# Folding and piece ends moved from VectorE to GpSimd, and one more border step with the border order, in a fused Fourier filter and SiLU network

## The chip, the core and the metric

The kernel runs on one core of one Trainium2 chip. Its time is the device time of one execution in microseconds (us), as the median of several runs. Before the change this is 2573.56 us (three runs, 2570.03 to 2574.13). The engines of the core work beside each other, each through its own instructions in order: PE (TensorE, matrix products), DVE (VectorE) and POOL (GpSimd) for elementwise work, ACT (ScalarE) for copies and SiLU, SP for issuing DMAs. POOL issues DMAs too, and such an issue stands in the same queue as its arithmetic.

## The reference

```python
X = np.fft.rfft(x, axis=1)                    # x: 8 x 3008 x 256, f32
y = np.fft.irfft(X * (filt_r + 1j * filt_i)[None], n=3008, axis=1)
h = y.reshape(8 * 3008, 256) @ w_in           # w_in: 256 x 2048
out = (h / (1 + np.exp(-h))) @ w_out          # w_out: 2048 x 256
```

Each of the 8 batches is filtered along its 3008 positions in the frequency domain. The 24064 tokens that result go through a two-layer network with SiLU.

## The kernel before

**The network is the frame.** A batch is cut into 6 pairs of token blocks (256, 256 and 240 columns, twice). For a pair, the 2048 hidden units are worked off in 8 steps (`jp` 0 to 7) of 256, so a batch has 48 steps and the kernel 384. Both matrix products of a step use a 2 by 2 scheme with seven block products in place of eight. `hidden(step)` issues the seven products with w_in (L957), ACT copies intermediate sums out of PSUM (L965, L972, L978) and does SiLU (L961), DVE combines (all through the helper `combine`, L928). `project(step)` issues the seven products with w_out (L1020) one step later (`LAG`), into four accumulators in PSUM, a0 to a3. At the end of a pair `drain` copies these to SBUF (L1038, L1040), POOL makes seven additions on them (L928, tile s), and SP stores them.

A step has 8 rounds. In each round PE gets one product of `hidden` and then one of `project` (round 5 has none of the former, round 7 none of the latter). Each product is two PE instructions. What follows calls the products by their weights: A11, A12, S2, S1, S3, then A22 and S4 for `hidden`. DVE's own work in a step is, in its order:

- g0: the sum of A12's result and a copy (it reads PSUM and SBUF), in round 1
- g6 and g7, in `finish`: differences within the tile g, for the step before (both operands in SBUF, 256 columns each); `project`'s sixth and seventh product, in rounds 5 and 6 of this step, read them
- g2, after S3, reads the bank that S4 will add to in round 7
- g1, after S4; the next step's A12 writes the bank that g1 reads
- g4 and g5 in one instruction: a difference within g, 512 columns, both operands in SBUF

**The filter is woven in.** The next batch's transform and filter and inverse transform are cut into pieces, and each is put by hand at a step and a round (`put(step, round, piece)`). After each round, pieces due by then are issued; they go into the engines' queues behind that round's work. For batches 2 to 7, `plan` and `plan_two` do this. Their times are relative to `at`, the batch's own first step (48 times its number):

- `fold(f, k)` (L486 to L499), three times (f 0 to 2) in four parts: sums and differences of x with its reversed copy, operands and results in SBUF, 120 partitions. Parts 0 and 1 are one instruction of 1024 columns each, parts 2 and 3 two of 512 each. f 0 is put at steps -68 to -66, f 1 at -60 to -58, f 2 at -52 to -50. The result is read by `stage1_fold` (PE, L509) at -64, -56 and -48, round 7, and `evict_fold` (ACT) and `pairs_fold` (DVE L444, L445; DMAs by POOL, L528) follow it.
- `load_fold` brings x_all in through SP nine steps ahead of f 0's product, and for f 1 and 2 after the previous product has read x_all. The fold's buffer "u" is single; for f 0 the last `multiply_two` (L586) of the batch before must have read it.
- `forward_two`, `multiply_two`, `add_two` (L591, L592), then `plan_inverse` for the groups g 0, 2 and 4: `inverse_two` (PE, L604), `even_two` (ACT), `rows_two` (DVE, two instructions on L616, one operand in PSUM), `ends_two` (DVE, L621 and L622, 512 columns each, both operands in SBUF), and two DMAs by POOL (L625). Each group has two such pieces, i 0 and 1. The inverse of a group is put at steps -32, -24 and -16 of its batch; its ends are at 2 and 3 steps after.
- `tokens(pair)` (DVE, three instructions "ty", SBUF to SBUF) is put once a pair. For the fifth pair of a batch it is due at step 26, round 6, which is the step of the ends of the next batch's group 2, piece 0 (26, round 5).

**Border steps.** At the first step of a pair (`jp` 0), filter pieces use accumulators that the pair before has just left. The set `joined` names steps at which `project` takes another order: A11, A12, S1, S3 before S4, so that a2 and a3 come late. At other borders S4 (which writes a2) comes first. The set `opened` issues two products of `project` ahead of `hidden`.

Of the kernel before, what the change touches and what calls it, by code (L numbers as in the profile page):

```python
# [49 lines left out]
ALU = mybir.AluOpType  # L50
# [177 lines left out]
def kernel(  # L228
# [9 lines left out]
    nc = tc.nc  # L238
# [95 lines left out]
    def spectral(b):  # L334
# [151 lines left out]
        def fold(f, k):  # L486

            used = slice(0, 120)
            if k == 0:
                us["f"] = upool.tile([128, 2, 512], FP32, name=f"uf_{b}_{f}", tag="u")  # L490
            xt, ut = x_all[used], us["f"][used]
            todo = (((ut, xt[:, :, 0], xt[:, :, 1], ALU.add),),
                    ((xt[:, :, 1], xt[:, :, 0], xt[:, :, 1], ALU.subtract),),
                    ((xt[:, 0, 0], ut[:, 0], ut[:, 1], ALU.add),
                     (xt[:, 1, 0], ut[:, 0], ut[:, 1], ALU.subtract)),
                    ((ut[:, 0], xt[:, 0, 1], xt[:, 1, 1], ALU.subtract),
                     (ut[:, 1], xt[:, 0, 1], xt[:, 1, 1], ALU.add)))
            for out, in0, in1, op in todo[k]:
                nc.vector.tensor_tensor(out=out, in0=in0, in1=in1, op=op)  # L499

        def stage1_fold(f):
            ut = us.pop("f")
# [115 lines left out]
        def ends_two(g, i):  # L618
            qt = halves[g][1][i]
            low = opool.tile([128, 2, C], FP32, name=f"low_{b}_{g}_{i}", tag="o")  # L620
            nc.vector.tensor_tensor(out=low, in0=qt[:, 0], in1=qt[:, 1], op=ALU.add)  # L621
            nc.vector.tensor_tensor(out=qt[:, 0], in0=qt[:, 0], in1=qt[:, 1], op=ALU.subtract)  # L622
            a0 = 8 * g + 8 * i
            for end, part in ((0, low), (1, qt[:, 0])):
                nc.gpsimd.dma_start(out=d2[a0:a0 + 8, 16 * end:16 * end + 16], in_=part)  # L625
# [146 lines left out]
    joined, opened = set(), set()  # L772
    ACCS, HIDDEN = (2, 3), ("x", "yz")

    def put(step, rnd, piece, *args):

        pending.append((step + rnd / ROUNDS, len(pending), lambda: piece(*args)))
# [3 lines left out]
    def plan(b, part):  # L781

        at = STEPS * b

        if b == 1:
            for u in range(2, 8):
                put(at + u - 49, 3, part["stage1"], u)
        else:
            put(at - 80, 0, part["reverse_x"])
            for f, step, load, places, ends in (  # L790
                    (0, -64, -73, ((-68, 3), (-68, 5), (-67, 5), (-66, 5)), ((1, 0), (1, 3))),
                    (1, -56, -63, ((-60, 3), (-60, 5), (-59, 5), (-58, 5)), ((1, 3), (1, 5))),
                    (2, -48, -55, ((-52, 3), (-52, 5), (-51, 5), (-50, 5)), ((1, 3), (1, 5)))):
                put(at + load, 0, part["load_fold"], f)
                for k, (fold_step, rnd) in enumerate(places):
                    put(at + fold_step, rnd, part["fold"], f, k)
                put(at + step, 7, part["stage1_fold"], f)
                put(at + step, 7, part["evict_fold"], f)
                for q, (after, rnd) in enumerate(ends):
                    put(at + step + after, rnd, part["pairs_fold"], f, q)  # L800
            opened.add(at - 63)
            for u, step in ((6, -46), (7, -45)):
                put(at - 47, 0, part["load_x"], u)
                put(at + step, 5, part["sums"], u)
            open_step(at - 44, (part["stage1"], 6), (part["stage1"], 7))
            put(at - 44, 3, part["pairs_t1"], 0)
            put(at - 44, 5, part["pairs_t1"], 1)
            return plan_two(b, part)
        put(at - 38, 0, part["load_t2"], 0)
        put(at - 38, 0, part["load_t2"], 1)  # L810
        for g, places in enumerate((
                ((-36, 3), (-36, 5), (-35, 3), (-35, 5), (-34, 5)),
                ((-35, 6), (-34, 3), (-33, 3), (-33, 5), (-32, 1)),
                ((-32, 7), (-31, 0), (-31, 2), (-28, 5), (-27, 2)),
                ((-27, 3), (-27, 5), (-26, 3), (-25, 3), (-24, 3)),
                ((-24, 7), (-23, 0), (-23, 2), (-20, 2), (-20, 5)),
                ((-20, 3), (-19, 3), (-19, 5), (-18, 3), (-18, 5)))):
            pieces = (("forward", g), ("multiply", g, 0), ("multiply", g, 1), ("add", g, 0), ("add", g, 1))
            for (step, rnd), (piece, *args) in zip(places, pieces):
                if piece != "forward" or g in (1, 3, 5):  # L820
                    put(at + step, rnd, part[piece], *args)
        open_step(at - 36, *last_part[0](5), (part["forward"], 0))
        for g, step in ((0, -32), (2, -24), (4, -16)):
            put(at + step, 7, part["inverse"], g, 2)
            if g < 4:
                pending.append((at + step + 7 / ROUNDS, 10 ** 6 + 9, lambda g=g: part["forward"](g + 2, ACCS)))
                joined.add(at + step)
            put(at + step, 7, part["even"], g, 0, 2)
            put(at + step, 7, part["even"], g, 1, 2)
            put(at + step + 1, 5, part["rows"], g, 0, 2)  # L830
            put(at + step + 2, 3, part["rows"], g, 1, 2)
        put(at - 14, 5, part["load_t4"], 0)
        put(at - 14, 5, part["load_t4"], 1)
        open_step(at - 10, *alone(part, 0), (part["stage3"], 1))
        put(at - 10, 3, part["evict_y"], 1, 0)
        put(at - 10, 5, part["evict_y"], 1, 1)
        join(at - 8, part, 2, 3)
        plan_rest(b, part)
# [11 lines left out]
    def plan_two(b, part):  # L850

        at = STEPS * b
        put(at - 42, 0, part["load_t2"], 0)
        put(at - 42, 0, part["load_t2"], 1)
        for g, step, places in (
                (0, -40, ((-39, 3), (-39, 5), (-38, 3), (-38, 5), (-37, 3), (-36, 3))),
                (2, -32, ((-31, 0), (-31, 2), (-29, 5), (-28, 3), (-28, 5), (-27, 3))),
                (4, -24, ((-23, 0), (-23, 2), (-22, 2), (-21, 5), (-20, 2), (-18, 3)))):
            if g:
                plan_inverse(at + step, part, g - 2)  # L860
                opened.add(at + step + 1)
            put(at + step, 7, part["forward_two"], g)
            put(at + step, 7, part["free_two"], g)
            pieces = (("multiply_two", 0, 0), ("multiply_two", 0, 1), ("add_two", 0),
                      ("multiply_two", 1, 0), ("multiply_two", 1, 1), ("add_two", 1))
            for (place, rnd), (piece, *args) in zip(places, pieces):
                put(at + place, rnd, part[piece], g, *args)
        plan_inverse(at - 16, part, 4)
        put(at - 12, 1, part["load_t4"], 0)
        put(at - 12, 1, part["load_t4"], 1)  # L870
        two_alone(at - 10, part, 0)
        join(at - 8, part, 2, 3)
        plan_rest(b, part)
# [7 lines left out]
    def open_step(step, *pieces):  # L881

        opened.add(step)
        for piece, *args in pieces:
            pending.append((step - 0.06, len(pending), lambda piece=piece, args=args: piece(*args)))

    def alone(part, g, home=HIDDEN):
        return (part["stage3"], g, home), (part["evict_y"], g, 1), (part["evict_y"], g, 0)
# [5 lines left out]
    def join(step, part, *gs):  # L894

        pieces = [(part["stage3"], gs[0], ACCS), (part["evict_y"], gs[0], 0)] if gs[0] is not None else []
        for g in gs[1:]:
            pieces = [*alone(part, g), *pieces]
        for k, (piece, *args) in enumerate(pieces):
            pending.append((step + 7 / ROUNDS, 10 ** 6 + k, lambda piece=piece, args=args: piece(*args)))  # L900
        if gs[0] is not None:
            put(step + 1, 0, part["evict_y"], gs[0], 1)
        joined.add(step)
# [458 lines left out]
    for b in range(1, B):  # L1362
        plan(b, second if b == 1 else spectral(b))
# [81 lines left out]
```

## Time and profile before

| What | Value |
|---|---|
| Median of 3 runs | 2573.56 us (2570.03 to 2574.13) |
| The profiled execution's own time | 2574.01 us |
| Its span (first to last instruction) | 2571.5 us |
| Granted clock of TensorE, mean | 0.996 |
| Busy: DVE, ACT, POOL | 1660.8, 1103.6, 438.5 us |
| Fold on DVE (L499), 72 of 512 columns and 36 of 1024 | 108 instructions, 90.2 us |
| Ends on DVE (L621, L622), all three groups | 72 instructions, 49.5 us |
| POOL's additions for the drains (L928, s) | 331 instructions, 256.1 us |

The busy time of an engine is the union of its instructions. A line of the timeline gives start, duration, engine, line, operation, and written tile "<-" read tiles with columns; several alike in a row are merged ("x2"). A bracket names the idle time before and who ended it. A line of the waits gives the waiting engine and instruction, who ended the wait, the total in us, the number of times and the longest.

### The profile page before, as it was taken

What the parts mean: (1) busy time and instruction counts of PE and PEld (TensorE: products, weight loads), DVE (VectorE), ACT (ScalarE), POOL (GpSimd) and SP (SyncE); (2) the same over time, 40 slices, a digit from 0 to 9 for tenths busy, and PEclk for the clock granted to TensorE, in tenths of its full rate; (3) what the DMA queues carried; (4) which work ended last, traced back from release to release, by engine and by line L of the source; (5) the groups of instructions that cost most, each with busy time, mean ns of one, the idle gap of its engine ahead of it and who ended that gap; (6) DMA issues with size and microseconds to landing.
All of it is one profiled execution on the core that took longest, in us unless ns stands there. A gap on an engine that the chain in (4) does not pass through costs nothing.

```text
span 2571.5 us, 47151 instructions
## 1 busy us (share of the span) xinstructions
PE 2531.8 (98%) x18810; PEld 2183.9 (85%) x18810; DVE 1660.8 (65%) x3451; ACT 1103.6 (43%) x3039; POOL 438.5 (17%) x682
## 2 busy tenths in 40 slices
PE   8999999999999999999999999999999999999998
PEld 6688788888888888888888888888888888888987
DVE  7866656577666776667766676666766666554544
ACT  3544344444444444444444444444444444444443
POOL 3211111022111111211121111211121111101101
PEclk9999999999999999999999999999999999999999
DMA  9622142222322222331324203332042211200000
GB/s 288 163 69 78 39 111 59 65 62 65 72 68 69 58 69 59 85 83 35 75 55 97 72 25 75 83 78 63 25 98 61 60 42 33 62 15 16 16 9 17
DMA packets 122740, 171.84 MB, mean 67 GB/s; under 512 B 20500, under 2 KB 96244, under 8 KB 121636
## 3 DMA queue, kind: packets, MB, share of 16 engines
q1 hardware_dynamic: 97352, 117.88, 18.0%
q0 software_dynamic: 22320, 45.80, 6.7%
q10 hardware_dynamic: 2848, 5.15, 0.7%
q8 instruction: 147, 2.41, 0.4%
q14 instruction: 73, 0.60, 0.1%
HBM read 96.91 MB, written 81.26 MB: 69 GB/s over the span
## 4 chain that ended last, share of the span: by engine, by line
PE 93%; DVE 3%; DMA 3%; ACT 1%; issue 0%; SPq 0%; ACTq 0%; POOL 0%; POOLq 0%; DVEq 0%
PE acc L1020 43%; PE px L957 25%; PE pyz L957 19%; PE pd L742 3%; PE pc L604 1%; PE pb L566 1%; DVE g L928 1%; PE pf L509 1%; DVE q L616 1%; PE pa L420 0%; DMA filt<-in_filt_i_dram 0%; DMA w_t<-in_x_dram 0%; DMA d<-q 0%; DMA w_t<-d 0%; DVE ty L928 0%
## 5 line engine op out<-in xcount | busy, mean ns | idle before, releaser
L1020 PE MATMUL acc<-g,w_t 128*128 128x256 f32 (+1 forms) x5376 | 1509.2, 375 | 2.8 <-DVE tf L445 2.4
L1020 PEld LDWEIGHTS acc<-g,w_t 128*128 128x128 f32 x5376 | 1020.6, 190 | 128.0 <-ACT q L610 9.5
L928 DVE TENSOR_TENSOR g<-pyz,abc 128x256 f32<-128x256 f32 (+1 forms) x1152 | 479.4, 416 | 612.0 <-ACT abc L978 335.9
L928 DVE TENSOR_TENSOR g<-g 128x256 f32<-128x256 f32 (+3 forms) x1152 | 592.9, 515 | 196.7 <-ACT g L961 183.6
L957 PE MATMUL px<-ty,w_t 128*128 128x256 f32 (+1 forms) x2304 | 678.0, 376 | 1.1 <-ACT abc L972 0.6
L961 ACT ACTIVATE g<-g 128x256 f32<-128x256 f32 (+1 forms) x1152 | 473.0, 411 | 259.2 <-DVE g L928 258.9
L928 POOL TENSOR_TENSOR s<-s 128x256 f32<-128x256 f32 (+1 forms) x331 | 256.1, 791 | 1654.5 <-DVE s L1038 1434.9
L957 PEld LDWEIGHTS px<-ty,w_t 128*128 128x128 f32 x2304 | 434.1, 190 | 59.9 <-ACT abc L972 3.9
L957 PE MATMUL pyz<-y,w_t 128*128 128x256 f32 (+1 forms) x1536 | 456.1, 379 | 10.9 <-DVE g L928 10.3
L957 PEld LDWEIGHTS pyz<-y,w_t 128*128 128x128 f32 x1536 | 282.0, 190 | 65.1 <-DVE g L928 26.6
L972 ACT COPY abc<-px 128x256 f32<-128x256 f32 (+1 forms) x384 | 141.3, 368 | 367.3 <-PE px L957 367.3
L978 ACT COPY abc<-px 128x256 f32<-128x256 f32 (+1 forms) x384 | 141.5, 369 | 319.3 <-PE px L957 319.1
L961 ACT ACTIVATE g<-px 128x256 f32<-128x256 f32 (+1 forms) x384 | 145.8, 380 | 298.4 <-PE px L957 298.4
L957 PE MATMUL px<-y,w_t 128*128 128x256 f32 (+1 forms) x768 | 231.3, 383 | 0.7 <-DVE y L756 0.7
L957 PE MATMUL pyz<-ty,w_t 128*128 128x256 f32 (+1 forms) x768 | 225.8, 376 | 0.2 <-DVE g L928 0.2
L957 PEld LDWEIGHTS px<-y,w_t 128*128 128x128 f32 x768 | 142.1, 190 | 25.4 <-ACT t L427 4.9
L957 PEld LDWEIGHTS pyz<-ty,w_t 128*128 128x128 f32 x768 | 143.3, 190 | 20.2 <-DVE g L928 1.0
L965 ACT COPY abc<-px 128x256 f32<-128x256 f32 (+1 forms) x384 | 135.2, 352 | 53.7 <-PE px L957 53.7
L1038 ACT COPY s<-acc 128x512 f32<-128x512 f32 (+1 forms) x94 | 54.2, 577 | 47.6 <-issue 28.5
L742 PEld LDWEIGHTS pd<-wn_t,t 48*64 48x64 f32 x3072 | 48.5, 135 | 16.6 <-ACT g L961 11.7
L625 POOL DMA_DIRECT2D d<-low x36 | 22.2, 618 | 194.0 <-DVE low L621 194.0
L742 PE MATMUL pd<-wn_t,t 48*64 48x47 f32 x3072 | 52.8, 232 | 1.2 <-issue 1.0
(157 smaller groups left out, 1346.8 us busy)
## 6 DMA issues: line engine op xcount, KB each, us to landing
t<-d SPq DMA_DIRECT2D x120, 192.0 KB
t<-d SPq DMA_DIRECT2D x84, 256.0 KB
out_dram<-s SPq DMA_DIRECT2D x64, 256.0 KB
d<-q POOLq DMA_DIRECT2D x48, 256.0 KB, 5.2
d<-low POOLq DMA_DIRECT2D x36, 256.0 KB, 4.2
xr<-in_x_dram SPq DMA_DIRECT2D x6, 1472.0 KB
out_dram<-s SPq DMA_DIRECT2D x30, 240.0 KB
x_all<-in_x_dram SPq DMA_DIRECT2D x72, 96.0 KB
```

The source lines that it names most:

```text
L509: nc.tensor.matmul(out=ps[q][32 * k:32 * k + 32], lhsT=wq_t[rows, k], rhs=rhs[k][rows], start=True, stop=True)
L566: nc.tensor.matmul(out=ps[k, ri][32 * j:32 * j + 32, a, :], lhsT=dn_t[rows, 4 * (g + a) + at, :], rhs=t2s[g + a][rows, at, :], start=True, ...
L604: nc.tensor.matmul(out=ps[j][cols, ri, :], lhsT=en_t[rows, g + a, k, ri, :], rhs=zs[k, ri][0][rows, a, :], start=True, stop=True)
L742: nc.tensor.matmul(out=ps[h][c0:c0 + 64, cb, 3 - i if back else i, :], lhsT=t4[rows, i, 128 * cb + c0:128 * cb + c0 + 64], rhs=table[rows, ...
L928: eng.tensor_tensor(out=out, in0=in0, in1=in1, op=op)
L957: nc.tensor.matmul(out=out, lhsT=w_t[:, jp, c, 0], rhs=rhs, start=start, stop=True, skip_group_check=True)
L961: nc.scalar.activation(out=g[:, k, 0:n], in_=g[:, k, 0:n] if src is None else src, func=AFT.Silu)
L965: nc.scalar.copy(out=sums[:, 0, 0:n], in_=xo)
L972: nc.scalar.copy(out=sums[:, 1, 0:n], in_=xo)
L978: nc.scalar.copy(out=sums[:, 2, 0:n], in_=xo)
L1020: nc.tensor.matmul(out=acc[pair][i][:, h, 0:n], lhsT=w_t[:, jp, c, 1], rhs=g[:, k, 0:n], start=(jp == 0 and h == 0), stop=last, skip_group ...
L1038: copy(out=s[:, 2 * i:2 * i + 2, 0:n], in_=acc[pair][i][:, :, 0:n])
```

## The change

The folding's instructions are issued by GpSimd. The ends of groups 0 and 2 are issued by GpSimd, those of group 4 stay on VectorE. Step `at - 64` joins the border order. For batch 2 that is step 32; for later batches the step (`at - 64` is 16 steps ahead of the first step of the batch before) is in the set already through `plan_inverse`, so only step 32 is new.

```diff
             for out, in0, in1, op in todo[k]:
-                nc.vector.tensor_tensor(out=out, in0=in0, in1=in1, op=op)
+                nc.gpsimd.tensor_tensor(out=out, in0=in0, in1=in1, op=op)
...
             low = opool.tile([128, 2, C], FP32, name=f"low_{b}_{g}_{i}", tag="o")
-            nc.vector.tensor_tensor(out=low, in0=qt[:, 0], in1=qt[:, 1], op=ALU.add)
-            nc.vector.tensor_tensor(out=qt[:, 0], in0=qt[:, 0], in1=qt[:, 1], op=ALU.subtract)
+            eng = nc.vector if g == 4 else nc.gpsimd
+            eng.tensor_tensor(out=low, in0=qt[:, 0], in1=qt[:, 1], op=ALU.add)
+            eng.tensor_tensor(out=qt[:, 0], in0=qt[:, 0], in1=qt[:, 1], op=ALU.subtract)
...
                     put(at + step + after, rnd, part["pairs_fold"], f, q)
+            joined.add(at - 64)
             opened.add(at - 63)
```

## The prediction

> **What bounds the kernel now.** I read the page's busy times first, then PE's waits over the whole span, then the timelines of DVE, POOL and PE around each wait.
>
> ```profile
> PE 2531.8 (98%) x18810; PEld 2183.9 (85%) x18810; DVE 1660.8 (65%) x3451; ACT 1103.6 (43%) x3039; POOL 438.5 (17%) x682
> ```
> ```profile
> PE pyz L957 <- DVE g L928: 10.5, 8, 1.6
> ...
> PE acc L1020 <- DVE tf L445: 2.4, 1, 2.4
> ```
>
> PE does not rest: what the change can win is what PE waits for DVE. Listing these waits in stretches of 20 us finds one of 1.6 at 584 us and one like it some 311 us later, five more times (one for each of batches 2 to 7), one of 0.6 at 280 to 287 us, where the fold of batch 2 stands ahead of a combine, and the 2.4 at 310.45 us, which is step 32's border. Everything else of DVE's 1660.8 us lies beside PE already. The wait at 584 us on DVE:
>
> ```profile
> 579.02 1.40 DVE L616 TENSOR_TENSOR q<-q,pc 128x512 f32<-128x512 f32 x2
> 580.35 0.42 DVE L928 TENSOR_TENSOR g<-pyz,abc 128x256 f32<-128x256 f32 x1
> 580.68 0.68 DVE L621 TENSOR_TENSOR low<-q 128x512 f32<-128x512 f32 x1
> 581.39 0.69 DVE L622 TENSOR_TENSOR q<-q 128x512 f32<-128x512 f32 x1
> 582.00 0.68 DVE L928 TENSOR_TENSOR ty<-y 128x512 f32<-128x512 f32 x1
> 582.72 0.88 DVE L928 TENSOR_TENSOR ty<-y,ty 128x256 f32<-128x256 f32 x2
> 583.52 0.42 DVE L928 TENSOR_TENSOR g<-pyz,abc 128x256 f32<-128x256 f32 x1
> ```
>
> The last line is g1; A12 of the next step starts at 584.00, 1.79 after its turn (the product before it began at 581.78 and products follow each other by 0.43). The ends in front cost g1 1.32 (580.68 to 582.00).
>
> **What POOL costs.** One addition of 256 columns alone takes 0.72 on POOL, one of 240 takes 0.69. From the two, 2.0 ns a column and 0.21 fixed: 1.25 for 512 columns, 2.3 for 1024 (DVE's rows: 0.68 and 1.23). In proportion to the columns it would be 1.45 and 2.9. No row shows POOL at these widths with two operands; I take the slope, as both its points are such additions, and keep the other as the upper end.
>
> **What POOL costs DVE.** This decides. In the drain at 414 us:
>
> ```profile
> 415.38 0.69 POOL L928 TENSOR_TENSOR s<-s 128x240 f32<-128x240 f32 x1
> 415.80 0.56 DVE L928 TENSOR_TENSOR g<-g 128x256 f32<-128x256 f32 x1
> 416.04 0.88 POOL L928 TENSOR_TENSOR s<-s 128x240 f32<-128x240 f32 x1
> 416.40 0.80 DVE L928 TENSOR_TENSOR g<-g 128x256 f32<-128x256 f32 x1
> ```
>
> g6 and g7 take 0.42 alone. Here the first ends at 416.36: it worked from 415.94, and the POOL instruction ended at 416.07. The second worked from 416.78 to 417.20, and its POOL instruction ended at 416.92. So where both operands of DVE lie in SBUF, DVE starts 0.14 before POOL ends, not earlier, and POOL in its turn is stretched (0.88 for 0.69). They alternate: the POOL instruction that waits goes in between g6 and g7. Combines that read PSUM keep 0.42 within such drains. In the drains a wait is 0.4 at most in such pairs, and PE shows no wait there. The trace has no longer POOL instruction against such a DVE one; the cost of a wait lies between 0.4 (as here) and nearly the whole instruction (1.1 at 512 columns, 2.2 at 1024). I take the whole one, since every stretched pair that I looked at starts at the same 0.14 before POOL's end, which is an order of turns, not a share.
>
> The Trainium skill ("SBUF — State Buffer", section "SBUF: two separate sides") states this as an exclusive lock held for the whole instruction, between GpSimd and DVE instructions with two SBUF inputs. The trace agrees at 256 columns and shows no wider pair. By the rule the sum is the one below; by a wait that stays at 0.4 it is the second rival's.
>
> **The folds, 18 of them.** POOL takes its queue in order, so fold 1 of batch 3 starts when the DMA issues ahead of it are done, at 639.9 us (its x has landed by then), near its place on DVE (643.67). The step there:
>
> ```profile
> 641.91 0.69 DVE L928 TENSOR_TENSOR g<-g 128x512 f32<-128x512 f32 x1 [0.48 <-ACT g L961]
> 642.52 0.42 DVE L928 TENSOR_TENSOR g<-pyz,abc 128x256 f32<-128x256 f32 x1
> 642.85 0.88 DVE L928 TENSOR_TENSOR g<-g 128x256 f32<-128x256 f32 x2
> 643.67 1.23 DVE L499 TENSOR_TENSOR uf<-x_all 120x1024 f32<-120x1024 f32 x1
> 645.29 0.42 DVE L928 TENSOR_TENSOR g<-pyz,abc 128x256 f32<-128x256 f32 x1 [0.39 <-ACT abc L978]
> ```
> ```profile
> 644.69 1.03 PE L1020 MATMUL acc<-g,w_t 128*128 128x256 f32 x4
> 645.55 0.59 PE L957 MATMUL px<-ty,w_t 128*128 128x256 f32 x2
> 645.98 0.59 PE L1020 MATMUL acc<-g,w_t 128*128 128x256 f32 x2
> 646.41 0.59 PE L957 MATMUL pyz<-y,w_t 128*128 128x256 f32 x2
> ```
>
> PE reads g6 at 645.12 (the second product in the first line), g7 at 645.98, and S4 at 646.41 wants g2 done. Walked with the turns above: POOL's first 1024 columns 639.95 to 642.26; g4 and g5 from 642.12 to 642.81; POOL's second 1024, effectively 642.67 to 644.98; g6 from 644.84 to 645.26; POOL's first 512 to 646.37; g7 from 646.23 to 646.65; g2 to 646.99. With 0.05 from DVE's end to PE, g6 costs 0.19 and g7 another 0.53: 0.72. The other 512s fit into the slack of the next step. The same walk for fold 0 (start 593.7, when the multiply that ends at 593.41 has read the buffer "u"; behind that wait POOL's queue holds only the fold's other parts and the drain at 619.65) gives 0.67, for fold 2 (start 687.0, after the DMA issues; 240 columns) 0.86. A restart of PE costs 0.1 more (0.53 from 584.00 to the next product in place of 0.43). Per batch 0.77 + 0.82 + 0.96 = 2.55, six batches **15.3**. DVE's 90.2 us of folding give nothing back but the 0.6 at 287, as PE waited nowhere else for it.
>
> **The ends.** Group 0 (530 us): each piece goes to POOL 0.29 after its rows (as the DMA issues follow theirs). The first takes 526.57 to 527.82, g4 and g5 wait from 527.07 to 527.68, the second goes in between, g6 starts at 529.31, the rows of the second piece end 1.4 later than now, g2 ends at 531.83 instead of 530.63, and S4, whose turn is 531.23, waits 0.65, with the restart 0.75; six times, **4.5**. Group 2 (584 us): the first piece delays g4 to g7 by 1.1 in the same way, so the rows end at 581.5 and g2 at 581.87. The ends of the second piece start on POOL at 581.8, when the three "ty" come: POOL 512, ty, POOL 512, ty, ty. "ty" end at 585.4, g1 at 585.78 instead of 583.95. The 1.32 taken off DVE return as two waits of 1.1 and the 1.1 from before: A12 starts **1.83 later than now**, not 1.79 earlier; six times, **11.0**. That the ends' DMAs leave some 2 us later is covered: group 2's rows are read from step -12, some 50 us on. SP's queue is not touched, and the additions of the drains have no fold ahead of them in POOL's queue that is still running.
>
> **Step 32.** S4 waits there for the pair (ACT 308.30, DVE 308.90 and 309.62, PE 310.45), 2.4 and 0.17 by the next product. In the new order A11 and A12 come first; their accumulators are free when ACT has copied the inverse's results, 306.87 + 1.07 = 307.94, before PE ends there at 308.30. The same border 311 us later, which has that order, shows PE busy 14.00 of 14.00 us. Gain **2.6** (bounds 0 and 2.6).
>
> **Sum** against the profiled execution: 2574.0 + 15.3 + 4.5 + 11.0 - 2.6 - 0.6 = 2601.6. The median was 0.45 lower than that execution: **2601 us**, 1.1% slower. With POOL at 1.45 and 2.9, the walk gives some 1.4 more per fold (25) and 1.2 per pair of groups and batch (7): 2633.
>
> **Rivals.**
>
> - POOL at the upper widths' cost: 2633. For: fixed costs on POOL are known from short instructions only. Against: the slope of 240 to 256.
> - POOL's long instructions let DVE in between (a wait stays under 0.4). Then folds cost nothing, as drains cost nothing now; at 584 us three or four waits of 0.4 eat what the ends gave; left are 2.6 + 0.6: 2571, and with no wait at all up to 1.3 x 6 more, 2563. For: no row shows a long instruction in the way. Against: the fixed 0.14. It decides from waits under about 1 us on g6 and g7 together, as these have 1.8 and 2.2 of slack in the step above. This is the side where the time is not slower.
> - The turns are as I say, but POOL starts in other phases, and half of the folds miss g6 and g7, with "ty" ahead of POOL: about 10 to 15 less, 2588.
>
> **How the numbers follow.** Forecast 0.47; other phases 0.18; upper cost 0.11; long instructions let DVE in 0.24, of which half ends within 0.2% (5 us, about what a measurement of this kernel can tell from no change) and half below. Slower 0.76, same 0.12, faster 0.12. Its own range is 2588 to 2633; to leave out no more than 2 in 10 the range reaches to 2563.
>
> **What would show it.** Right: DVE's g<-g of 256 columns stretched to 1 to 2.5 us beside folds; new waits of PE acc on DVE g; the six waits of pyz at 3 us or more, or waits at S4 beside them; tf's 2.4 gone; POOL's 512s at 1.25 and 1024s at 2.3 unstretched. Wrong: g<-g beside folds below 0.9, or the six waits below 1.

## The result, and the profile after

The changed kernel takes **2614.0 us** (median of 4 runs, 2612.84 to 2616.36) against 2571.9 us before (4 runs): a ratio of **1.0165** (95% interval 1.0147 to 1.0182), 1.65% slower. The profiled execution took 2612.84 us, its span is 2611.0, 39.5 more than before. The page's first line of engines, and PE's waits over the whole span:

```profile
PE 2547.4 (98%) x18810; PEld 2183.1 (84%) x18810; DVE 1647.2 (63%) x3295; ACT 1108.0 (42%) x3039; POOL 694.8 (27%) x838
```
```profile
PE pyz L959 <- DVE g L930: 31.6, 23, 4.1
PE acc L1022 <- DVE g L930: 5.7, 21, 0.4
```

DVE has 156 instructions less, but only 13.6 us less busy time, although the moved ones took 90.2 + 33 us before: the rest of DVE's instructions have become longer. PE waits for DVE's combines 44 times, where it waited 8 times for pyz and once for acc, and the wait for tf at step 32 is gone. (The helper's line L928 is L930 here.) The groups of POOL by shape:

```profile
L499 POOL TENSOR_TENSOR uf<-x_all 120x512 f32<-120x512 f32 x36 | 50.7, 1430 | 1.4
L499 POOL TENSOR_TENSOR x_all<-x_all 120x1024 f32<-120x1024 f32 x18 | 46.2, 2568 | 1.4
L499 POOL TENSOR_TENSOR uf<-x_all 120x1024 f32<-120x1024 f32 x18 | 42.4, 2357 | 53.8 <-PE px L959 51.0 <-DMA x_all<-xr 1.1 <-DMA out_dram<-s 1.0
L622 POOL TENSOR_TENSOR low<-q 128x512 f32<-128x512 f32 x24 | 30.4, 1265 | 64.6 <-DVE q L616 64.6
```

1024 columns take 2.35 where nothing is in the way and 512 take 1.27; where a mean is longer than that, POOL has itself waited for DVE's turn. The 64.6 of idle time ahead of the ends were all ended by DVE's rows (q, L616): POOL starts the ends as soon as the rows are done.

The place at 584 us of before, now near 589. DVE's and POOL's timelines:

```profile
579.69 0.97 DVE L930 TENSOR_TENSOR g<-g 128x512 f32<-128x512 f32 x1 [0.48 <-ACT g L963]
580.92 1.62 DVE L930 TENSOR_TENSOR g<-g 128x256 f32<-128x256 f32 x2
...
585.32 1.65 DVE L930 TENSOR_TENSOR ty<-y 128x512 f32<-128x512 f32 x1
587.00 1.83 DVE L930 TENSOR_TENSOR ty<-y,ty 128x256 f32<-128x256 f32 x2
588.75 0.41 DVE L930 TENSOR_TENSOR g<-pyz,abc 128x256 f32<-128x256 f32 x1
```
```profile
578.85 1.27 POOL L622 TENSOR_TENSOR low<-q 128x512 f32<-128x512 f32 x1 [4.02 <-DVE q L616]
580.19 1.60 POOL L623 TENSOR_TENSOR q<-q 128x512 f32<-128x512 f32 x1
...
585.15 1.27 POOL L622 TENSOR_TENSOR low<-q 128x512 f32<-128x512 f32 x1 [2.21 <-DVE q L616]
586.50 1.59 POOL L623 TENSOR_TENSOR q<-q 128x512 f32<-128x512 f32 x1
```

The first "ty" of 512 columns began on paper at 585.32, but ends at 586.97, 0.55 after the POOL instruction that ended at 586.42: taking its own 0.68, it worked from 586.29, 0.13 before that end. The second pair shows the same. PE waits twice here, 1.10 ahead of S4 and 2.20 ahead of A12:

```profile
585.45 0.70 PE L959 MATMUL pyz<-y,w_t 128*128 128x256 f32 x2 [1.10 <-DVE g L930]
589.22 0.70 PE L959 MATMUL pyz<-y,w_t 128*128 128x256 f32 x2 [2.20 <-DVE g L930]
```

Where the 39.5 comes from, by the start of the same product of PE in both traces (a difference that grows is time lost there): 7.1 at the first fold of batch 2; 1.45 at each later first fold and 0.9 at each second (1.5 in batch 2), of which 0.45 and 0.2 come back nearby, where DVE no longer folds; 1.1 to 1.3 at each third; 0.9 at each of the six ends of group 0 and 1.6 at those of group 2, with 1.7 more behind three of these. Won are 1.6 between 280 and 294 us and 3.8 at step 32. Some 1.8 of the startup (up to 85 us) went the other way, which is no part of the change. What is left, about 2 us, is a sum of single steps of up to 1.0 either way whose cause is not known.

### The profile page after: what moved, and what is told of

Read it like the earlier page. It is cut to its first block, busy times and chain, and to the rows that moved or that the text cites. A ratio compares the mean times of both kernels' runs of the same rounds, so it can differ in the third digit from the quotient of the medians.

```text
span 2611.0 us, 47225 instructions
## 1 busy us (share of the span) xinstructions
PE 2547.4 (98%) x18810; PEld 2183.1 (84%) x18810; DVE 1647.2 (63%) x3295; ACT 1108.0 (42%) x3039; POOL 694.8 (27%) x838
## 4 chain that ended last, share of the span: by engine, by line
PE 86%; DVE 8%; DMA 2%; issue 2%; ACT 1%; ACTq 0%; SPq 0%; POOL 0%; POOLq 0%; DVEq 0%
PE acc L1022 39%; PE px L959 23%; PE pyz L959 17%; DVE g L930 5%; PE pd L743 3%; DVE q L616 1%; DVE ty L930 1%; PE pc L604 1%; PE pb L566 1%; PE pf L509 1%; ACT g L963 1%; PE pa L420 0%; DMA w_t<-in_x_dram 0%; DMA d<-q 0%; DMA filt<-in_filt_r_dram 0%
## 5 line engine op out<-in xcount | busy, mean ns | idle before, releaser
L930 DVE TENSOR_TENSOR g<-pyz,abc 128x256 f32<-128x256 f32 (+1 forms) x1152 | 479.4, 416 | 667.1 <-ACT abc L980 337.1
L930 DVE TENSOR_TENSOR g<-g 128x256 f32<-128x256 f32 (+3 forms) x1152 | 679.2, 590 | 196.8 <-ACT g L963 183.6
L930 POOL TENSOR_TENSOR s<-s 128x256 f32<-128x256 f32 (+1 forms) x331 | 256.9, 794 | 1476.2 <-ACT s L1040 739.2
L499 POOL TENSOR_TENSOR uf<-x_all 120x512 f32<-120x512 f32 (+1 forms) x54 | 93.2, 1739 | 55.2 <-PE px L959 51.0
```

What stands on the lines that cost most here:

```text
L499: nc.gpsimd.tensor_tensor(out=out, in0=in0, in1=in1, op=op)
L930: eng.tensor_tensor(out=out, in0=in0, in1=in1, op=op)
```

## The experiments

Theory: while POOL works on operands in SBUF, a DVE instruction with both operands in SBUF waits to the end of POOL's instruction, and PE waits where DVE's slack is smaller than that. Rivals: the ends beside "ty" are all of it; DVE is slowed in proportion to POOL's work; the results of POOL come late. (No PE wait on POOL's folds or ends stands in the trace after, which speaks against the last.) All ratios are to the kernel before, run on the same chip; microseconds more or less are worked out from the ratio, not from the medians.

### The border order alone

```diff
+            joined.add(at - 64)
             opened.add(at - 63)
```

> The border order at step 32 alone. Theory: the wait of 2.4 us there goes, and with it the half clock that follows it in the trace of before (0.57 granted from 310 to 314 us): 3.8 us less than before, ratio 0.9985. Rival (the prediction's own term): 2.6 us less, and the clock after it plays no part. Second rival: another wait takes its place and the time stays.

Measured: 2569.7 us, ratio 0.9983 (0.9974 to 0.9993), 4.4 us less with an interval of 1.8 to 6.7. The timing alone can't tell 3.8 from 2.6. The trace can: PE is busy 6.00 of 6.00 us from 308 to 314 us at full clock. Busy time and granted clock in two stretches, before and then this kernel (us, PE, PEld, DVE, ACT, POOL, clock, DMA share, GB/s):

```profile
308.00:310.00 2.00, 0.04 (x2) 0.00 (x0) 1.07 (x2) 1.07 (x2) 1.92 (x3) 1.00 0.34 111
310.00:314.00 4.00, 3.55 (x9) 2.92 (x10) 0.30 (x1) 0.37 (x1) 0.16 (x1) 0.57 0.67 141
```
```profile
308.00:310.00 2.00, 2.00 (x10) 1.55 (x10) 1.93 (x5) 0.72 (x3) 1.05 (x2) 1.00 0.72 189
310.00:314.00 4.00, 4.00 (x20) 3.51 (x19) 3.68 (x7) 1.84 (x6) 2.08 (x5) 1.00 0.62 130
```

In the second stretch before, PE looks busy, but runs 9 instructions (two make a product) instead of 20: it waits to 310.45, and the granted clock is 0.57. By the products' starts this border gains 3.8.

### The folds alone by GpSimd

```diff
-                nc.vector.tensor_tensor(out=out, in0=in0, in1=in1, op=op)
+                nc.gpsimd.tensor_tensor(out=out, in0=in0, in1=in1, op=op)
```

> Folding alone by GpSimd. Theory (VectorE's instructions with both operands in SBUF wait for the end of the whole GpSimd instruction): about 23 us more than before: 7 at the first fold of batch 2, where the three instructions ty stand in front of g1, and about 1 for each of the other 17, less 2 from VectorE's relief near 287 us; ratio 1.009. Rival (the loss lies in the ends beside ty alone): within 3 us of before. The wait of 1.6 us near 584 us stays in both.

Measured: 2601.0 us, ratio 1.0103 (1.0089 to 1.0117), 26.5 more (22.9 to 30.1). The rival falls. The wait of 4.1 near 269 us, those of 1.2 at the later first folds, and 20 short ones of acc (5.7 together) are in this trace too, beside the six old ones of 1.6:

```profile
PE pyz L957 <- DVE g L928: 21.9, 18, 4.1
PE acc L1020 <- DVE g L928: 5.7, 20, 0.4
```

### The ends of groups 0 and 2 alone by GpSimd

The second hunk of the change, without the others.

> The ends of groups 0 and 2 alone by GpSimd. Theory: per batch about 1 us at group 0 and 1.6 at group 2, six times 16, and some 1.7 us of half clock after group 2's wait in some of the batches: 16 to 26 us more than before, ratio 1.006 to 1.010. Rival (the ends gain as meant, the folds lose): 8 us less than before.

Measured: 2593.0 us, ratio 1.0072 (1.0056 to 1.0089), 18.5 more (14 to 23). In place of six waits of 1.6 stand six of 1.1 and six of 2.2, as in the trace after. Half clock follows two of them here.

```profile
PE pyz L958 <- DVE g L929: 21.0, 15, 2.2
```

The three parts add up to 40.6, the whole change measured 42.

### The folds by GpSimd, in pieces of 256 columns

```diff
-                nc.vector.tensor_tensor(out=out, in0=in0, in1=in1, op=op)
+                for a in range(2 if k < 2 else 1):
+                    for c in range(0, 512, 256):
+                        cut = [(t[:, a] if k < 2 else t)[:, c:c + 256] for t in (out, in0, in1)]
+                        nc.gpsimd.tensor_tensor(out=cut[0], in0=cut[1], in1=cut[2], op=op)
```

> Folding alone by GpSimd, each instruction cut into pieces of 256 columns (16 a fold in place of 6, about 11.6 us of GpSimd work in place of 9.6). Theory (a wait lasts to the end of one GpSimd instruction): no wait over 0.6 us, VectorE's slack takes them, and the time is within 3 us of before, g<-g of 256 columns not over 1.1 us. Rival (GpSimd's work slows VectorE in proportion to its sum, whatever its pieces): as much as the uncut folds or more, 20 us or more over before.

Measured: 2672.4 us, ratio **1.0385** (1.0364 to 1.0406), 99 more. The theory as I had stated it falls here: short pieces made it far worse. The longest instruction of DVE in that trace, and the POOL pieces beside it:

```profile
265.96 11.30 DVE L931 TENSOR_TENSOR ty<-y,ty 128x256 f32<-128x256 f32 x1
```
```profile
266.05 2.76 POOL L502 TENSOR_TENSOR uf<-x_all 120x256 f32<-120x256 f32 x4
268.77 2.76 POOL L502 TENSOR_TENSOR x_all<-x_all 120x256 f32<-120x256 f32 x4
271.50 2.76 POOL L502 TENSOR_TENSOR x_all<-uf 120x256 f32<-120x256 f32 x4
274.22 2.76 POOL L502 TENSOR_TENSOR uf<-x_all 120x256 f32<-120x256 f32 x4
```

An instruction of 0.42 took 11.30: it waited for all 16 pieces, and worked from 0.14 before the end of the last. In nine of the 18 folds a DVE instruction was shut out so, for some 5 to 11 us, in the other nine it got its turn after one piece. But proportion to POOL's work is no better an account: 16 pieces of 0.69 are 11 us a fold, where the uncut fold takes 10.6 ((50.7 + 50.7 + 46.2 + 42.4) / 18), and the loss is nearly four times as large. PE's waits for DVE in this trace:

```profile
PE pyz L960 <- DVE g L931: 81.2, 21, 10.6
```

Nine of them, of 4.8 to 10.6, one for each chain that shut DVE out, make 70 of the 99. The rest goes with the slower clock behind them: the granted clock is 0.982 on the mean, against 0.996 before.

What sets these pieces apart: none has to wait. In the uncut folds, three of the five instructions behind the first have to wait for the one in front (part 1 writes what part 0 reads), so that POOL pauses; the cut pieces need one that is two or four back and done. New theory: DVE gets its turn for certain where POOL's next instruction has to wait.

### The same pieces in another order

```diff
+            if k % 2 == 0:
+                us["todo"] = todo[k]
+                return
+            for a in range(2 if k < 2 else 1):
+                for c in range(0, 512, 256):
+                    for out, in0, in1, op in (*us["todo"], *todo[k]):
+                        cut = [(t[:, a] if k < 2 else t)[:, c:c + 256] for t in (out, in0, in1)]
+                        nc.gpsimd.tensor_tensor(out=cut[0], in0=cut[1], in1=cut[2], op=op)
```

Part 0's pieces are issued with part 1's, and part 2's with part 3's, so that a piece follows the one it depends on.

> The folds by GpSimd in the same 16 pieces of 256 columns as in e4_split, but in another order, in which pieces wait for the piece in front of them: every second one in the first half of a fold, every fourth in the second half. Theory (VectorE gets its turn only where GpSimd's next instruction has to wait, or now and then between two; a chain of 16 that never waits shuts it out): no wait over 3 us, time within 6 us of before. Rival (short GpSimd instructions at full rate shut VectorE out in whatever order): 50 us or more over before, as e4_split.

Measured: 2578.7 us, ratio 1.0014 (1.0006 to 1.0023), 3.6 more. Same pieces, same work: the order differs, and with it the moment at which parts 0 and 2 are issued, and 95 us go. That moment does not explain it: in both traces POOL starts the folds at the same place. Batch 3's first two start 9.6 and 56.4 us behind the old wait of group 2 (607.6 us) in the trace of the fourth experiment, and 9.5 and 56.6 behind the same wait (583.7) here. The same "ty" as above and POOL's pieces beside it:

```profile
264.91 1.11 DVE L934 TENSOR_TENSOR ty<-y,ty 128x256 f32<-128x256 f32 x1
266.05 0.83 DVE L934 TENSOR_TENSOR ty<-y,ty 128x256 f32<-128x256 f32 x1
```
```profile
264.99 0.74 POOL L505 TENSOR_TENSOR uf<-x_all 120x256 f32<-120x256 f32 x1
265.81 0.80 POOL L505 TENSOR_TENSOR x_all<-x_all 120x256 f32<-120x256 f32 x1
266.56 0.90 POOL L505 TENSOR_TENSOR uf<-x_all 120x256 f32<-120x256 f32 x1
```

No wait of DVE is over 0.7 us. That also shows what the folds' place on DVE is worth: with the 90 us of folding off DVE, PE's products come 1.6 earlier near 285 us and 0.2 at several later folds, and the turns that are left (1.3 at the first fold, 0.7 at each later batch's first) use that up.

### The changed kernel with "ty" elsewhere

```diff
-    combines = ((-2, 1), (6, 1), (11, 5), (22, 5), (26, 6), (38, 1))
+    combines = ((-2, 1), (6, 1), (11, 5), (22, 5), (31, 1), (38, 1))
```

> The changed kernel with the tokens of a batch's fifth pair at step 31, round 1, instead of step 26, round 6, and nothing else. Theory (ty in turns with GpSimd is what group 2's ends cost, and ty beside the first fold of batch 2 what that one costs): 6 us less at that fold, 1.8 us less at each of six ends, and 5 us of half clock gone: 2592, ratio to before 1.008. Rival (the waits of g4 to g7 alone make the loss, ty matters little): 2605 or more.

Measured: 2589.6 us, ratio 1.0052 (1.0036 to 1.0067). The waits of 4.1 and 2.2 are gone and no half clock remains between 100 us and the end; the waits of 1.1 ahead of S4, of 1.2 at the first folds and the short ones of acc stay:

```profile
PE pyz L959 <- DVE g L930: 14.1, 15, 1.2
PE acc L1022 <- DVE g L930: 5.8, 21, 0.4
```

Against the whole change that is 0.0113 of the base, 29 us less. Not all of it is POOL's: without POOL the same move of "ty" brings 12 (0.9983 to 0.9936, the first experiment against the next). So some 17 us lie in the meeting of POOL with "ty", and 30 (0.9936 to 1.0052) in what POOL still does elsewhere.

### Border order and "ty" elsewhere, all arithmetic on VectorE

The line of the first experiment and that of the last.

> Folds and ends stay on VectorE; the border order at step 32, and the tokens of a batch's fifth pair at step 31, round 1, instead of step 26, round 6. Theory (PE's waits of 1.6 us come from ends and ty in one row on VectorE): the six waits go, 6 x 1.9, and 3.8 at step 32: 15 us less than before, ratio 0.994, the fastest so far. Rival: the row is too long without ty as well, the waits shrink to about half: 9 us less.

Measured: 2560.1 us, ratio **0.9936** (0.9924 to 0.9949), the fastest of all. PE's waits in this trace:

```profile
PE pyz L958 <- DVE g L929: 1.2, 3, 0.6
PE acc L1021 <- DVE g L929: 0.4, 1, 0.4
```

The 10.5 of before have become 1.2, by moving three instructions of DVE to a place some five steps later, not to another engine.

## Why the prediction was right

The direction, the mechanism and the range held; the loss was put at 27.6 and is 38.8 between the profiled executions. Step by step:

**What POOL costs.** Right: 1.25 and 2.3 by the slope, 1.27 and 2.35 measured.

**What POOL costs DVE.** Right for this kernel: waits last to 0.14 before the end of POOL's instruction at 512 and 1024 columns too. In the clearest case DVE takes 2.73 and 2.44 for 0.42 each; in the walked step of fold 1, g6 takes 2.24 and g7 1.37:

```profile
649.35 2.24 DVE L930 TENSOR_TENSOR g<-g 128x256 f32<-128x256 f32 x1
651.62 1.37 DVE L930 TENSOR_TENSOR g<-g 128x256 f32<-128x256 f32 x1
```

As a general statement ("an order of turns") it was too kind: the turns are certain only where POOL pauses, as the fourth experiment showed. The rival that POOL's long instructions let DVE in falls.

**The folds.** The walk of fold 1 gave 0.82 with PE's restart, and 0.9 was measured; fold 2 gave 0.96, measured 1.1 to 1.3. Fold 0 of batches 3 to 7 gave 0.77 and came to 1.45, some 1.0 after the 0.45 that the freed DVE returns: there g4 and g5 wait 1.75 and push g0 back, and PE's S1 waits for g0, a reader that the walk left out. **The term that failed is fold 0 of batch 2**, which I had counted like the others at 0.77 without walking it. Its buffer is free early, so POOL takes it at 263.59, 12 us ahead of DVE's place for it (275.29), beside "ty":

```profile
262.79 0.68 DVE L930 TENSOR_TENSOR ty<-y 128x512 f32<-128x512 f32 x1
263.51 5.21 DVE L930 TENSOR_TENSOR ty<-y,ty 128x256 f32<-128x256 f32 x2
268.64 0.41 DVE L930 TENSOR_TENSOR g<-pyz,abc 128x256 f32<-128x256 f32 x1
```

PE waits 4.07 for that g1, and with the half clock behind it 7.1 are lost: 6.3 more than the 0.77 counted.

**The ends.** Group 0: 0.75 predicted, 0.9 measured, and that it is so near is luck. The forecast had one wait of 0.65 at S4; measured are three delays, of 0.2 at S1 (531.23 us, for g0), 0.3 at S4 (534.38, for g2) and 0.4 at the next step's S1 (537.59, for g0 again). Group 2: 1.83 predicted, 1.6 measured, in the two places foretold (S4 and A12). The 1.7 behind three of the six were not counted; see below.

**Step 32.** 2.6 predicted, 3.8 measured; the mechanism was right, and the half clock after the wait was missed here too, to the other side.

**The sum.** What was left out is the clock: after the change it drops in four places, before in one. In the three behind group 2's ends it costs 1.7 each, at batch 2's first fold 2.8, and the 1.7 at step 32 go with its wait: some 6 us net. The wait at fold 0 of batch 2, which the walk left out, is some 3.5 more than counted. Together these are nearly all of the missing 11; the smaller misses, to both sides, about cancel.

The rival of other phases (fewer losses) found no support: the places repeat from batch to batch within some tenths, as the steps do. That of POOL's upper widths' cost falls with the measured widths, though its time (2633) is 19 above the measured median and the forecast 13 below it.

**What stays open.** What decides whether a DVE instruction gets in between two POOL instructions that need not wait. In the kernel before and after it always did between two such; in chains of 16 it was shut out in half of the folds. The moment of arrival may decide; no run here sets it apart.

## What to carry to other kernels

An engine's busy share says nothing of what relieving it will bring: look for the instructions ahead of those that the bounding engine waits for, and move them in time before moving them to another engine. Work moved to GpSimd is not beside VectorE's work but in turn with it wherever both operands of VectorE lie in SBUF; count a whole GpSimd instruction for each such VectorE instruction that stands on the path, and remember that GpSimd starts when its data allow, not where the code puts it on VectorE. If such work must go there, cut it short and let pieces depend on the one in front (here every second to fourth did), so that VectorE gets in; in this kernel even that won nothing (1.0014).

## What the runs showed of the hardware

- A chain of 16 GpSimd instructions that need not wait kept a VectorE instruction of 0.42 us out for 10.9 us. The Trainium skill ("SBUF — State Buffer", section "Summary: rules for kernel authors") gives the rule by the single instruction: the second one to issue blocks until the first has finished. The 256-column runs differ: the wait can be longer than one instruction, and the measurement decides.
- A wait of PE costs more than itself. Granted clock behind the wait of 2.20 in batch 4, in the trace after:

```profile
905.00:907.00 2.00, 0.97 (x3) 0.79 (x4) 1.48 (x4) 0.68 (x2) 1.05 (x2) 0.82 0.32 33
907.00:910.00 3.00, 3.00 (x10) 2.38 (x9) 1.33 (x4) 0.69 (x2) 0.00 (x0) 0.55 0.48 153
910.00:914.00 4.00, 4.00 (x20) 3.53 (x19) 2.05 (x4) 1.40 (x5) 0.00 (x0) 1.00 0.01 2
```

  The clock missing there is 0.18 x 2 + 0.45 x 3 = 1.7 us, that is 3.4 us at half. The same waits of 1.10 and 2.20 bring it in three of six batches after, in two of six with the ends alone. The Trainium skill ("TensorE: Matmul & The Clock Gate", section "Part 1: The HAM clock gate (the "warmup" mystery)") tells of free-running windows of about 3.4 us, of which an idle one halves the clock and a busy one restores it; the length agrees with these rows, and here 2.03 us of idle time in a window were enough. The stretches of half clock in the trace after begin at 267.97, 906.26, 1541.14 and 2176.02 us, which lie 187, 186 and 186 times 3.413 us apart. That grid decides which of the equal waits are punished. Cut at its marks, batch 4 (the first two lines) and batch 5 read:

```profile
902.85:906.26 3.41, 1.21 (x6) 0.76 (x5) 3.05 (x4) 0.26 (x1) 3.12 (x4) 1.00 0.14 41
906.26:909.67 3.41, 3.41 (x9) 2.67 (x9) 1.87 (x4) 1.11 (x4) 0.00 (x0) 0.50 0.53 137
1220.29:1223.70 3.41, 1.56 (x6) 1.06 (x6) 3.38 (x4) 0.42 (x1) 2.98 (x3) 1.00 0.31 95
1223.70:1227.11 3.41, 2.40 (x11) 2.15 (x12) 2.70 (x7) 1.37 (x4) 1.03 (x2) 1.00 0.44 93
```

  In batch 4 the wait of 2.20 lies in one window, PE is idle there for 2.20 of 3.41 us, and the next window runs at half. In batch 5 a mark divides the wait, the two windows have 1.85 and 1.01 of idle time, and the clock stays. In the nine traces of this case, between 100 us and the last 12 us, each of the 21 windows at full clock with 2.03 us or more of idle PE was followed by half clock, and none with 1.95 or less was.
- Each restart of PE after a wait costs 0.1 us beside the wait (0.53 to the next product instead of 0.43).
